# An attention stage rearranged: heads paired four apart, the spectrum stored mode-innermost, one cast moved to GpSimd, weight loads moved behind q, k, v

## The chip, the cores and the metric

The kernel runs on one core of a Trainium2 chip. The metric is device time in microseconds (us) for one execution; lower is better. A NeuronCore has a matrix engine (PE, TensorE), a vector engine (DVE, VectorE), an activation engine (ACT, ScalarE), GpSimd (POOL), a sync engine (SP) and sixteen DMA engines. Each engine takes its instructions in the order in which they were queued; an instruction that waits holds those behind it.

## The reference

Linear attention with phi(x) = elu(x) + 1, for 8 batches, 8 heads, 576 positions and 64 channels per head. Its output, laid out as 576 x 512 per batch, goes through a spectral mix: a real Fourier transform over positions, of which 64 modes are kept, a complex 512 x 512 matrix per mode, the inverse transform, and a residual channel product.

```python
q_p, k_p = (phi(q), phi(k))
kv = np.einsum('bhsd,bhse->bhde', k_p, v)
z = np.sum(k_p, axis=2)
num = np.einsum('bhsd,bhde->bhse', q_p, kv)
den = np.einsum('bhsd,bhd->bhs', q_p, z)[..., None] + 1e-06
x = (num / den)            # heads side by side: 512 channels

X = np.fft.rfft(x, axis=1)
Yr = einsum('bmd,mde->bme', Xr, w_r) - einsum('bmd,mde->bme', Xi, w_i)   # modes 0..63
Yi = einsum('bmd,mde->bme', Xr, w_i) + einsum('bmd,mde->bme', Xi, w_r)
y = np.fft.irfft(Y, n=S, axis=1)
u = x + y
return u + np.maximum(u @ w_ch, 0.0)
```

All inputs and the output are float32 in HBM. The weights w_r and w_i are 64 MB each.

## The kernel before, in words

**Attention stage, batch after batch.** Three loads on GpSimd's queue (line 141) bring k, q and v of a batch, cast to half precision on the way, into tiles of a pool with five buffers ("raw"). A tile is 128 partitions by four head pairs by 576: the 128 partitions hold two heads of 64 rows, and a head pair is two neighbouring heads. For k and for q, ACT takes the exponential in two halves (line 163), DVE makes max(x, 0) + 1 in place (line 164), and two DVE minima combine the two into phi (line 168). v is copied beside a column of ones (line 171). On PE, 36 small matmuls form k-transposed times v (kvp, line 182); ACT copies the wanted blocks (kvs, line 192); q is transposed in two groups of nine (line 204), each copied out by ACT (qT, line 209). For four groups of 128 positions and a tail of 64, PE forms numerator and denominator (num, line 228); DVE takes the reciprocal (line 235) and multiplies in two instructions of 256 columns (line 239) into the float32 tiles x_main and x_tail, which the kernel keeps to the end. ACT casts two groups at a time to half precision (line 248, 1024 columns) and the tail by itself (line 246). PE then applies the forward transform (xf, lines 254 and 257), and the spectrum goes into the tile xt_c.

**The spectrum tile.** xt_c is, for each of four channel groups, a run of modes; in a mode stand three sets of eight batches: minus the imaginary part (t = 0), the real part (t = 1) and the imaginary part (t = 2). DVE writes t = 1 and t = 2 (lines 260 and 261), ACT writes t = 0 with a factor of -1 (line 262). Each writes single elements 24 apart.

**Mode products.** For each mode two weight tiles (wr, wi, half a MB each when cast) are loaded (line 119). Eight matmuls multiply 32 neighbouring columns of xt_c, as the stationary operand, with 512 columns of weights (lines 319, 278 and 284). Of the 32 result rows of each channel group, sixteen count: `pick` selects them in a further matmul (lines 294 and 362). A stage tile (ystage, three buffers) takes the product out of PSUM.

**Weight buffers.** Modes 0 and 1 have a pool of four tiles, modes 2 to 6 the first use of a pool of ten; the load for mode 7 needs a buffer that the product of mode 2 hands back. Batch b of the attention stage issues the loads of mode b - 1, so that seven modes are asked for by batch 7; wch, the channel weights, follows (line 299).

**The rest.** Between the mode products, 36 channel products of x are made (line 340 on). At the end the inverse transform, the sums and the stores run (from line 415 on).

**The order of the work.** The program names an engine for each instruction. A planner sets the order of each engine's queue when the kernel is built, by program order and by its own estimate of when operands and buffers are ready; a load may thus stand ahead of one that comes earlier in the program. On the chip that order is fixed. PSUM has eight banks: three buffers of two banks ("big": kvp, the two transposes and num) and two for xf.

Of the kernel before, what the change touches and what calls it, by code (L numbers as in the profile page):

```python
# [20 lines left out]
def _dft_consts(S: int, NM: int):  # L21

    p = np.arange(NP)
    m = np.arange(NM)
    fwd = np.zeros((128, 5, 2 * NM), dtype=np.float64)
    s_cols = np.empty(S, dtype=np.int64)
    for jj in range(4):
        for j2 in range(2):
            s = NJ * p + 2 * jj + j2
            ang = 2.0 * np.pi * np.outer(s, m) / S  # L30
            fwd[j2 * 64 : j2 * 64 + 64, jj, :NM] = np.cos(ang)
            fwd[j2 * 64 : j2 * 64 + 64, jj, NM:] = -np.sin(ang)
# [12 lines left out]
    inv[:, 1, :] = -np.sin(ang) * scale[:, None]  # L45
    pick = np.zeros((128, 16), dtype=np.float16)
    for quad in range(4):
        for c in range(16):
            pick[quad * 32 + 8 + c, c] = 1.0
    return fwd.astype(np.float16), inv.reshape(2 * NM, S).astype(np.float16), pick  # L50


# [1 line left out]
def kernel(  # L54
# [10 lines left out]
    nc = tc.nc  # L65
# [4 lines left out]
    NHP = H // 2  # L70
    NDC = D // 128
    NJJ = 4
    SLOT = 3 * B
    XTW = 8 + NM * SLOT + 8
    NL = 8
    NE = NM - NL

# [27 lines left out]
        xpool.tile([128, D], F32, tag="x_tail", bufs=B // 2, name=f"x_tail{i}")  # L105
        for i in range(B // 2)
    ]
    xt_c = xpool.tile([128, NDC, XTW], BF16, name="xt_c")
    nc.vector.memset(xt_c[:, :, 0:8], 0.0)
    nc.vector.memset(xt_c[:, :, XTW - 8 : XTW], 0.0)  # L110
    xt_v = xt_c[:, :, 8 : 8 + NM * SLOT].rearrange("p c (m t b) -> p c m t b", t=3, b=B)

    W_KEEP = 10

# [21 lines left out]

    for b in range(B):
        raw = {}
        for nm, src in (("k", k), ("q", q), ("v", v)):
            t = sA.tile([128, NHP, NJ * Dh], F16, tag="raw", bufs=5, name=f"{nm}16_{b}")  # L140
            nc.gpsimd.dma_start(
                out=t,
                in_=src[b].rearrange("h s d -> (h s) d").rearrange(
                    "(hp r j) d -> r hp (j d)", r=128, j=NJ
                ),
            )
            raw[nm] = t
        if b >= 1:
            kk = b - 1
            if kk < n_pre:  # L150
                w_in[kk] = w_load(kk, wpre, "wp", W_PRE)
            else:
                w_in[kk] = w_load(kk, wpool, "w", W_KEEP)

        phi = {}
        for nm in ("k", "q"):

            e = sA.tile([128, 2, NJ, 2, Dh], F16, tag=f"{nm}e", bufs=2, name=f"{nm}e_{b}")
            ev = e.rearrange("p c j o d -> p c o j d")
            rf = raw[nm].rearrange("p a f -> p (a f)")  # L160
            rv = raw[nm].rearrange("p (c o) (j d) -> p c o j d", o=2, d=Dh)
            for c in range(2):
                nc.scalar.activation(out=ev[:, c], in_=rv[:, c], func=AF.Exp)  # L163
            nc.vector.tensor_scalar(  # L164
                out=rf, in0=rf, scalar1=0.0, scalar2=1.0, op0=ALU.max, op1=ALU.add
            )
            for c in range(2):
                nc.vector.tensor_tensor(out=ev[:, c], in0=ev[:, c], in1=rv[:, c], op=ALU.min)  # L168
            phi[nm] = e
# [48 lines left out]
        for jj in range(NJJ + 1):  # L218
# [3 lines left out]
            for hpp in range(2):  # L222
                for h2 in range(2):
                    for hpo in range(2):
# [8 lines left out]
            nv = num[orow, :, 0:260].rearrange("p o (c t n) -> p c o t n", c=2, t=2)  # L233
            rden = sA.tile([128, 2, 2, 2], F32, tag="rden", bufs=3, name=f"rd{b}_{jj}")
            nc.vector.reciprocal(out=rden[orow], in_=nv[:, :, :, :, 64])
            dst = xtl[orow, :] if tail else xm[:, jj, :]
            dv = dst.rearrange("p (c o t d) -> p c o t d", c=2, o=2, t=2)
            for hpp in range(2):
                nc.vector.tensor_tensor(
                    out=dv[:, hpp],  # L240
                    in0=nv[:, hpp, :, :, 0:64],
                    in1=rden[orow, hpp].unsqueeze(3).broadcast_to([64 if tail else 128, 2, 2, Dh]),
                    op=ALU.mult,
                )
            if tail:
                nc.scalar.copy(out=x16t[orow, :], in_=dst)
            elif jj % 2 == 1:
                nc.scalar.copy(out=x16[:, jj - 1 : jj + 1, :], in_=xm[:, jj - 1 : jj + 1, :])  # L248

        xf = psA.tile([128, NDC, 2, NM], F32, tag="xf", bufs=2, name=f"xf{b}")  # L250
        for dc in range(NDC):
# [5 lines left out]
            nc.tensor.matmul(  # L257
                o, x16t[half, dc::NDC], fwd_sb[half, NJJ, :], start=False, stop=True
            )
        nc.vector.tensor_copy(out=xt_v[:, :, :, 1, b], in_=xf[:, :, 0, :])  # L260
        nc.vector.tensor_copy(out=xt_v[:, :, :, 2, b], in_=xf[:, :, 1, :])
        nc.scalar.mul(out=xt_v[:, :, :, 0, b], in_=xf[:, :, 1, :], mul=-1.0)

    n_in = len(w_in)

# [6 lines left out]
    def mode_product(kk: int, ps, stage, yt_ps):  # L272
# [3 lines left out]
        for dc in range(NDC):  # L276
            quad = slice(dc * 32, dc * 32 + 32)
            nc.tensor.matmul(  # L278
                P[quad, :], xt_c[:, dc, 8 + kk * SLOT : 8 + kk * SLOT + 32], wr[:, dc, :],
                start=True, stop=False, tile_position=(0, dc * 32),  # L280
            )
        for dc in range(NDC):
            quad = slice(dc * 32, dc * 32 + 32)
            nc.tensor.matmul(  # L284
                P[quad, :], xt_c[:, dc, kk * SLOT : kk * SLOT + 32], wi[:, dc, :],
                start=False, stop=True, tile_position=(0, dc * 32),
            )
        st = stage.tile([128, D], F16, tag="ystage", bufs=3, name=f"ys{kk}")
        if kk % 2 == 0:
            nc.vector.tensor_copy(out=st, in_=P)  # L290
        else:
# [20 lines left out]
    for kk in range(n_pre):  # L312
        wr, wi = w_get(kk)
        P = psA.tile([128, D], F32, tag="xf", bufs=2, name=f"P{kk}")
        for t, w in ((0, wr), (1, wi)):
            for dc in range(NDC):
                quad = slice(dc * 32, dc * 32 + 32)
                c0 = kk * SLOT + (8 if t == 0 else 0)
                nc.tensor.matmul(
                    P[quad, :], xt_c[:, dc, c0 : c0 + 32], w[:, dc, :],  # L320
                    start=(t == 0), stop=(t == 1), tile_position=(0, dc * 32),
                )
        st = ystage0.tile([128, D], F16, tag="ystage", bufs=3, name=f"ys{kk}")
        if kk % 2 == 0:
            nc.vector.tensor_copy(out=st, in_=P)
        else:
# [169 lines left out]
```

## Time and profile before

| | |
|---|---|
| median of 3 runs | 487.29 us (486.23 to 487.69) |
| profiled execution: time | 487.18 us |
| profiled execution: span | 485.2 us |
| DVE busy | 171.2 us, 35% of the span |
| ACT busy | 163.5 us, 34% |
| PE busy, weight loads | 255.5 us (53%), 129.4 us (27%) |
| GpSimd busy | 108.6 us, 22% |
| DMA | 92.20 MB, mean 190 GB/s; GpSimd's queue 81.80 MB |
| chain that ended last | DMA 65%, issue 13%, DVE 8%, PE 7%, ACT 4% |

How to read the rows: a row of a timeline has the start in us from the span's start, the duration, the engine, the line, the operation, output and inputs with partitions x elements, the count, and in brackets the idle time of the engine before it with what ended it. A count over 1 merges neighbours; the duration is then that of all. A row of the groups ends in: busy us, mean ns of one | idle us before it and what ended most of it. A DMA issue row ends in KB and us from issue to landing. A row of one line of the kernel ends in the least, median and largest duration in ns, and the first and last start. The slice rows split the span into forty equal parts; a digit is the busy share in tenths, 9 for 90% or more.

### The profile page before, as it was taken

What the parts mean: (1) busy time and instruction counts of PE and PEld (TensorE: products, weight loads), DVE (VectorE), ACT (ScalarE), POOL (GpSimd) and SP (SyncE); (2) the same over time, 40 slices, a digit from 0 to 9 for tenths busy, and PEclk for the clock granted to TensorE, in tenths of its full rate; (3) what the DMA queues carried; (4) which work ended last, traced back from release to release, by engine and by line L of the source; (5) the groups of instructions that cost most, each with busy time, mean ns of one, the idle gap of its engine ahead of it and who ended that gap; (6) DMA issues with size and microseconds to landing.
All of it is one profiled execution on the core that took longest, in us unless ns stands there. A gap on an engine that the chain in (4) does not pass through costs nothing.

```text
span 485.2 us, 5542 instructions
## 1 busy us (share of the span) xinstructions
PE 255.5 (53%) x2156; PEld 129.4 (27%) x2156; DVE 171.2 (35%) x337; ACT 163.5 (34%) x227; POOL 108.6 (22%) x173
## 2 busy tenths in 40 slices
PE   0344576556747675677675433232323359429870
PEld 0333444434522322233332100010000028303320
DVE  1667667877452212211211101010110012116992
ACT  3657667874533434344334100000000002102320
POOL 3412313200003222222222222222222222003561
PEclk9957655565557979988979755555555559757996
DMA  9999999990006999999999999999999999962995
GB/s 160 211 209 209 209 211 209 211 209 17 1 0 121 213 214 213 213 214 213 214 213 214 213 214 214 213 213 212 215 212 215 212 215 211 215 124 75 283 274 171
DMA packets 37739, 92.20 MB, mean 190 GB/s; under 512 B 3537, under 2 KB 16593, under 8 KB 37713
## 3 DMA queue, kind: packets, MB, share of 16 engines
q0 software_dynamic: 31632, 81.80, 86.9%
q1 hardware_dynamic: 3328, 5.20, 3.6%
q10 hardware_dynamic: 2752, 4.85, 3.2%
q8 instruction: 17, 0.28, 0.2%
q14 instruction: 10, 0.07, 0.0%
HBM read 163.93 MB, written 9.44 MB: 357 GB/s over the span
## 4 chain that ended last, share of the span: by engine, by line
DMA 65%; issue 13%; DVE 8%; PE 7%; ACT 4%; POOL 0%; POOLq 0%; SPq 0%; DVEq 0%
DMA q_3_640<-in_q_dram 4%; DMA wi_3418<-in_moe_w_i_dram 4%; DMA wr_2621<-in_moe_w_r_dram 4%; DMA wr_3283<-in_moe_w_r_dram 4%; DMA wr_3109<-in_moe_w_r_dram 4%; DMA wr_2988<-in_moe_w_r_dram 4%; DMA wr_2865<-in_moe_w_r_dram 4%; DMA wr_2500<-in_moe_w_r_dram 4%; DMA wr_2256<-in_moe_w_r_dram 4%; DMA wr_2133<-in_moe_w_r_dram 4%; DMA wr_2012<-in_moe_w_r_dram 4%; DMA wr_2744<-in_moe_w_r_dram 4%; DMA wr_2377<-in_moe_w_r_dram 4%; DMA wr_1889<-in_moe_w_r_dram 4%; DMA k_5_998<-in_k_dram 4%
## 5 line engine op out<-in xcount | busy, mean ns | idle before, releaser
L284 PEld LDWEIGHTS <-xt_c 128*32 128x32 bf16 x248 | 11.8, 101 | 86.1 <-issue 84.9
L278 PEld LDWEIGHTS <-xt_c 128*32 128x32 bf16 x248 | 9.0, 98 | 44.9 <-issue 17.9
L119 POOL DMA_DIRECT2D wr_1732<-in_moe_w_r_dram x1 | 0.5, 543 | 51.0 <-PE P_1627 L278 51.0
L182 PE MATMUL kvp_121<-vpad_100,ke_108 64*128 64x130 f16 x36 | 2.1, 308 | 15.2 <-DVE vpad_100 L171 15.2
L382 PEld LDWEIGHTS <-YT 128*112 128x112 f16 x32 | 7.7, 288 | 2.7 <-issue 2.2
L441 POOL TENSOR_TENSOR x_main_76<-x_main_76,r_3474 128x512 f32<-128x512 f32 x1 | 1.3, 1267 | 29.6 <-ACT r_3474 L440 29.6
L388 PEld LDWEIGHTS <-YT 128*112 128x112 f16 x32 | 7.5, 294 | 0.5
L182 PEld LDWEIGHTS <-ke_108 64*128 64x128 f16 x36 | 2.0, 141 | 15.1 <-DVE ke_108 L168 12.6
L424 PEld LDWEIGHTS <-inv_sb 128*128 128x128 f16 x32 | 3.2, 100 | 8.7 <-issue 6.6
L419 PEld LDWEIGHTS <-id_64 128*128 128x128 f16 x36 | 3.5, 100 | 6.4 <-issue 2.1
L423 PEld LDWEIGHTS <-inv_sb 128*128 128x128 f16 x32 | 3.3, 102 | 4.8 <-issue 1.7
L163 ACT ACTIVATE ke_108<-k_0_102 128x1152 f16<-128x1152 f16 x2 | 2.2, 1154 | 6.5 <-DMA k_0_102<-in_k_dram 6.5
L254 PE MATMUL xf_254<-fwd_sb,x_0_184 128*128 128x128 f16 x16 | 2.2, 263 | 4.0 <-ACT x_0_184 L248 4.0
L164 DVE TENSOR_SCALAR k_0_102<-k_0_102 128x2304 f16<-128x2304 f16 x1 | 0.8, 759 | 9.9 <-ACT ke_108 L163 9.9
L163 ACT ACTIVATE ke_468<-k_2_458 128x1152 f16<-128x1152 f16 x2 | 2.3, 1160 | 5.6 <-DMA k_2_458<-in_k_dram 5.6
L292 ACT CAST ys_3429<-P_3420 128x512 f16<-128x512 f32 x1 | 0.6, 586 | 10.4 <-PE P_3420 L284 10.4
L290 DVE CAST ys_3410<-P_3401 128x512 f16<-128x512 f32 x1 | 0.7, 691 | 9.4 <-PE P_3401 L284 9.4
L163 ACT ACTIVATE ke_828<-k_4_818 128x1152 f16<-128x1152 f16 x2 | 2.7, 1326 | 3.9 <-DMA k_4_818<-in_k_dram 3.9
L290 DVE CAST ys_2810<-P_2801 128x512 f16<-128x512 f32 x1 | 0.7, 692 | 9.1 <-PE P_2801 L284 9.1
L290 DVE CAST ys_3122<-P_3113 128x512 f16<-128x512 f32 x1 | 0.7, 691 | 9.1 <-PE P_3113 L284 9.1
L290 DVE CAST ys_2931<-P_2922 128x512 f16<-128x512 f32 x1 | 0.7, 692 | 9.1 <-PE P_2922 L284 9.1
L290 DVE CAST ys_2687<-P_2678 128x512 f16<-128x512 f32 x1 | 0.7, 691 | 9.1 <-PE P_2678 L284 9.1
(1293 smaller groups left out, 844.5 us busy)
## 6 DMA issues: line engine op xcount, KB each, us to landing
k_0_102<-in_k_dram POOLq DMA_DIRECT2D x1, 576.0 KB, 7.5
q_0_104<-in_q_dram POOLq DMA_DIRECT2D x1, 576.0 KB, 9.4
v_0_106<-in_v_dram POOLq DMA_DIRECT2D x1, 576.0 KB, 11.5
k_1_278<-in_k_dram POOLq DMA_DIRECT2D x1, 576.0 KB, 13.6
q_1_280<-in_q_dram POOLq DMA_DIRECT2D x1, 576.0 KB, 15.7
v_1_282<-in_v_dram POOLq DMA_DIRECT2D x1, 576.0 KB, 9.2
k_2_458<-in_k_dram POOLq DMA_DIRECT2D x1, 576.0 KB, 14.7
q_2_460<-in_q_dram POOLq DMA_DIRECT2D x1, 576.0 KB, 15.7
```

Of the source, the lines that this page charges most:

```text
L163: nc.scalar.activation(out=ev[:, c], in_=rv[:, c], func=AF.Exp)
L182: nc.tensor.matmul(kv_ps[:, h2, hpp * 130 : hpp * 130 + 130], kp[rows, hpp, j].rearrange("p o d -> p (o d)"), vp[rows, 2 * hpp : 2 * hpp + ...
L254: nc.tensor.matmul(o, x16[:, jj, dc::NDC], fwd_sb[:, jj, :], start=(jj == 0), stop=False)
L278: nc.tensor.matmul(P[quad, :], xt_c[:, dc, 8 + kk * SLOT : 8 + kk * SLOT + 32], wr[:, dc, :], start=True, stop=False, tile_position=(0, dc ...
L284: nc.tensor.matmul(P[quad, :], xt_c[:, dc, kk * SLOT : kk * SLOT + 32], wi[:, dc, :], start=False, stop=True, tile_position=(0, dc * 32),)
L290: nc.vector.tensor_copy(out=st, in_=P)
L382: nc.tensor.matmul(z_ps[: 2 * NE, :], lhs, wch16[:, ec, :], start=(ec == 0), stop=(ec == NDC - 1),)
L388: nc.tensor.transpose(y_ps[: 2 * NE, ec * 128 : ec * 128 + 128], lhs, id16)
L419: nc.tensor.matmul(e, id16, E0[t], start=True, stop=False, skip_group_check=True)
L423: nc.tensor.matmul(y, lhs, YZ[b][:, 0, :])
L424: nc.tensor.matmul(e, lhs, YZ[b][:, 1, :], start=False, stop=True, skip_group_check=True)
L441: nc.gpsimd.tensor_tensor(out=x, in0=x, in1=r, op=ALU.add)
```

## The change

Four things in the attention stage and one in what reads the spectrum.

1. Heads are paired four apart: the pair (c, o) is head pair c plus two times o, where it was two times c plus o. Views of the raw tiles and of v change accordingly. In num, the eight heads then stand so that one DVE multiplication of 512 columns writes a whole group of positions.
2. The cast of x to half precision (128 x 512 per group of positions) is issued to GpSimd, one group at a time, instead of to ACT for two groups. The tail's cast stays on ACT.
3. xt_c is stored with the mode as the innermost index: group, t, batch, mode. One DVE copy writes t = 1 and t = 2 together in runs of 64; ACT's negation writes runs of 64. The 32 stationary columns of a mode are now 64 elements (128 bytes) apart; a pad of 1024 elements at the end is cleared. `pick` moves by eight rows.
4. q is loaded and processed ahead of k. Weight loads are issued in batches 2, 4 and 6 only (modes 0, 1, 2); those of modes 3 to 6 come in the loop behind wch that was there already.
5. ystage has two buffers instead of three.

```diff
-    SLOT = 3 * B
-    XTW = 8 + NM * SLOT + 8
+    XDC = 3 * B * NM
+    XTW = NDC * XDC + 2 * B * NM
...
-    xt_c = xpool.tile([128, NDC, XTW], BF16, name="xt_c")
-    nc.vector.memset(xt_c[:, :, 0:8], 0.0)
-    nc.vector.memset(xt_c[:, :, XTW - 8 : XTW], 0.0)
-    xt_v = xt_c[:, :, 8 : 8 + NM * SLOT].rearrange("p c (m t b) -> p c m t b", t=3, b=B)
+    xt_c = xpool.tile([128, XTW], BF16, name="xt_c")
+    nc.vector.memset(xt_c[:, NDC * XDC : XTW], 0.0)
+    xt_v = xt_c[:, 0 : NDC * XDC].rearrange("p (c t b m) -> p c t b m", c=NDC, t=3, b=B)
+
+    def xt_cols(dc: int, t: int, kk: int):
+
+        c0 = dc * XDC + t * B * NM + kk
+        return xt_c[:, c0 : c0 + 31 * NM + 1 : NM]
...
-        for nm, src in (("k", k), ("q", q), ("v", v)):
+        for nm, src in (("q", q), ("k", k), ("v", v)):
...
-        if b >= 1:
-            kk = b - 1
+        if b % 2 == 0 and b > 0:
+            kk = b // 2 - 1
...
-        for nm in ("k", "q"):
+        for nm in ("q", "k"):
...
-            rv = raw[nm].rearrange("p (c o) (j d) -> p c o j d", o=2, d=Dh)
+            rv = raw[nm].rearrange("p (o c) (j d) -> p c o j d", o=2, d=Dh)
...
-                        vp[rows, 2 * hpp : 2 * hpp + 2, j, 0:65],
+                        vp[rows, hpp::2, j, 0:65],
...
-            for hpp in range(2):
-                nc.vector.tensor_tensor(
-                    out=dv[:, hpp],
-                    in0=nv[:, hpp, :, :, 0:64],
-                    in1=rden[orow, hpp].unsqueeze(3).broadcast_to([64 if tail else 128, 2, 2, Dh]),
-                    op=ALU.mult,
-                )
+            nc.vector.tensor_tensor(
+                out=dst.rearrange("p (o c d) -> p o c d", o=2, c=4),
+                in0=nv[:, :, :, 0:64],
+                in1=rden[orow].unsqueeze(3).broadcast_to([64 if tail else 128, 2, 4, Dh]),
+                op=ALU.mult,
+            )
             if tail:
                 nc.scalar.copy(out=x16t[orow, :], in_=dst)
-            elif jj % 2 == 1:
-                nc.scalar.copy(out=x16[:, jj - 1 : jj + 1, :], in_=xm[:, jj - 1 : jj + 1, :])
+            else:
+                nc.gpsimd.tensor_copy(out=x16[:, jj, :], in_=dst)
...
-        nc.vector.tensor_copy(out=xt_v[:, :, :, 1, b], in_=xf[:, :, 0, :])
-        nc.vector.tensor_copy(out=xt_v[:, :, :, 2, b], in_=xf[:, :, 1, :])
-        nc.scalar.mul(out=xt_v[:, :, :, 0, b], in_=xf[:, :, 1, :], mul=-1.0)
+        nc.vector.tensor_copy(out=xt_v[:, :, 1:3, b, :], in_=xf)
+        nc.scalar.mul(out=xt_v[:, :, 0, b, :], in_=xf[:, :, 1, :], mul=-1.0)
...
-                P[quad, :], xt_c[:, dc, 8 + kk * SLOT : 8 + kk * SLOT + 32], wr[:, dc, :],
+                P[quad, :], xt_cols(dc, 1, kk), wr[:, dc, :],
...
-                P[quad, :], xt_c[:, dc, kk * SLOT : kk * SLOT + 32], wi[:, dc, :],
+                P[quad, :], xt_cols(dc, 0, kk), wi[:, dc, :],
...
-        st = stage.tile([128, D], F16, tag="ystage", bufs=3, name=f"ys{kk}")
+        st = stage.tile([128, D], F16, tag="ystage", bufs=2, name=f"ys{kk}")
```

More of the change, by code (lines that the diff above doesn't have):

```diff
@@ L48, in _dft_consts @@
         for c in range(16):
-            pick[quad * 32 + 8 + c, c] = 1.0
+            pick[quad * 32 + c, c] = 1.0
     return fwd.astype(np.float16), inv.reshape(2 * NM, S).astype(np.float16), pick
@@ L232 @@
                         )
[L233 to L235 removed]
+            nv = num[orow, :, 0:260].rearrange("p o (c n) -> p o c n", c=4)
+            rden = sA.tile([128, 2, 4], F32, tag="rden", bufs=3, name=f"rd{b}_{jj}")
+            nc.vector.reciprocal(out=rden[orow], in_=nv[:, :, :, 64])
             dst = xtl[orow, :] if tail else xm[:, jj, :]
[L237 to L244 removed]
+            nc.vector.tensor_tensor(
[4 more added lines that the diff above has]
+            )
             if tail:
                 nc.scalar.copy(out=x16t[orow, :], in_=dst)
[L247 to L248 removed]
+            else:
+                nc.gpsimd.tensor_copy(out=x16[:, jj, :], in_=dst)
         xf = psA.tile([128, NDC, 2, NM], F32, tag="xf", bufs=2, name=f"xf{b}")
@@ L317 @@
                 quad = slice(dc * 32, dc * 32 + 32)
-                c0 = kk * SLOT + (8 if t == 0 else 0)
                 nc.tensor.matmul(
-                    P[quad, :], xt_c[:, dc, c0 : c0 + 32], w[:, dc, :],
+                    P[quad, :], xt_cols(dc, 1 - t, kk), w[:, dc, :],
                     start=(t == 0), stop=(t == 1), tile_position=(0, dc * 32),
                 )
-        st = ystage0.tile([128, D], F16, tag="ystage", bufs=3, name=f"ys{kk}")
+        st = ystage0.tile([128, D], F16, tag="ystage", bufs=2, name=f"ys{kk}")
         if kk % 2 == 0:
```

## The prediction

> **What bounds the kernel now.** I read the page first: its forty slices, then the group with the longest idle time.
>
> ```profile
> span 485.2 us, 5542 instructions
> DMA  9999999990006999999999999999999999962995
> L119 POOL DMA_DIRECT2D wr_1732<-in_moe_w_r_dram x1 | 0.5, 543 | 51.0 <-PE P_1627 L278 51.0
> ```
>
> The DMA engines are full except for a hole of three slices of 12.1 us. The hole ends with the load wr_1732, which waits for a product of mode 2 to hand back a weight buffer. So I read the GpSimd queue and the DMA issues around it.
>
> ```profile
> 97.15 0.75 POOL L141 DMA_DIRECT2D v_7_1362<-in_v_dram  x1 [4.65 <-issue]
> 148.86 0.54 POOL L119 DMA_DIRECT2D wr_1732<-in_moe_w_r_dram  x1 [50.96 <-PE P_1627 L278]
> ...
> v_7_1362<-in_v_dram POOLq DMA_DIRECT2D x1, 576.0 KB, 14.0
> wr_1732<-in_moe_w_r_dram POOLq DMA_DIRECT2D x1, 512.0 KB, 5.1
> ```
>
> The last load before the hole lands at 97.15 + 14.0 = 111.15. By then all q, k, v, wch and seven modes' weights are in, and every weight buffer is taken. Nothing moves until the attention stage ends and the products of modes 0 to 2 run. After that the chain of waits is DMA, load after load:
>
> ```profile
> 160.50 19.13 DMA wr_1889<-in_moe_w_r_dram
> ...
> 180.16 19.13 DMA wr_2012<-in_moe_w_r_dram
> ```
>
> Eight loads go by between the first two issues: 19.66 / 8 = 2.46 us for one. This stretch keeps its length whatever the attention stage does. So the span moves one for one with the issue of wr_1732, now at 148.86. A hole closed entirely would put wr_1732's own 2.46 us behind 111.15, instead of landing at 148.86 + 5.1: a gain of 40.4, the floor at 487.2 - 40.4 = 446.8.
>
> The question is then what the attention stage takes. Its spectrum matmuls close each batch:
>
> ```profile
> L257 PE MATMUL xf_254<-fwd_sb,x16t_185 x4: 244/245/292, 36.1 to 37.9; 64*128 64x128 f16 x4
> ...
> L257 PE MATMUL xf_1334<-fwd_sb,x16t_1265 x4: 291/292/307, 125.5 to 127.9; 64*128 64x128 f16 x4
> ...
> L257 PE MATMUL xf_1514<-fwd_sb,x16t_1445 x4: 291/292/295, 138.4 to 140.7; 64*128 64x128 f16 x4
> ```
>
> Batch 0 ends at 38.1, batch 6 at 128.2, batch 7 at 141.0: 14.7 us a batch on average, but 12.9 for the last, when no load is outstanding. The ACT timeline has the difference:
>
> ```profile
> 8.73 2.21 ACT L163 ACTIVATE ke_108<-k_0_102 128x1152 f16<-128x1152 f16 x2 [6.50 <-DMA k_0_102<-in_k_dram]
> 11.54 2.22 ACT L163 ACTIVATE qe_114<-q_0_104 128x1152 f16<-128x1152 f16 x2 [0.59 <-DMA q_0_104<-in_q_dram]
> ...
> 30.78 1.16 ACT L163 ACTIVATE ke_468<-k_2_458 128x1152 f16<-128x1152 f16 x1 [5.63 <-DMA k_2_458<-in_k_dram]
> 31.84 1.03 ACT L248 CAST x_0_184<-x_main_76 128x1024 f16<-128x1024 f32 x1
> ```
>
> ACT holds at the exponential of k of batch b+2 until that tensor lands, and batch b's cast to half precision stands behind it. The tensors land 11.54 - 8.73 = 2.81 us apart.
>
> **The change part by part.** I follow the last batch, from the end of xf_1334 (128.15):
>
> ```profile
> 128.19 1.33 DVE L260 CAST xt_c<-xf_1334 128x256 bf16<-128x256 f32 x1 [4.11 <-PE xf_1334 L257]
> ...
> 133.42 0.21 DVE L235 RECIPROCAL rd_0_1455<-num_0_1446 128x8 f32<-128x8 f32 x1 [2.72 <-PE num_0_1446 L228]
> ...
> 133.66 0.76 DVE L239 TENSOR_TENSOR x_main_83<-num_0_1446,rd_0_1455 128x256 f32<-128x256 f32 x2
> ```
>
> ```profile
> 128.22 0.75 ACT L192 CAST kvs_1418<-kvp_1381 64x260 f16<-64x260 f32 x2 [3.44 <-PE xf_1334 L257]
> 129.32 1.12 ACT L209 COPY qT_1421<-qTp_0_1422 128x1152 f16<-128x1152 f16 x1 [0.34 <-PE qTp_0_1422 L204]
> 130.73 1.34 ACT L262 ACTIVATE xt_c<-xf_1334 128x256 bf16<-128x256 f32 x1 [0.29 <-DVE xt_c L261]
> 131.55 1.47 ACT L209 COPY qT_1421<-qTp_1_1433 128x1152 f16<-128x1152 f16 x1
> ...
> 136.68 1.04 ACT L248 CAST x_7_1444<-x_main_83 128x1024 f16<-128x1024 f32 x1 [0.47 <-DVE x_main_83 L239]
> 137.75 0.62 ACT L246 CAST x16t_1445<-x_tail_87 64x512 f16<-64x512 f32 x1
> 143.66 1.34 ACT L262 ACTIVATE xt_c<-xf_1514 128x256 bf16<-128x256 f32 x1 [5.30 <-DVE xt_c L261]
> 147.61 0.62 ACT L342 CAST x16w_1687<-x_main_76 128x512 f16<-128x512 f32 x1
> ```
>
> Spectrum stored mode-innermost. Lines 260, 261 and 262 now write every 24th element; they become one DVE copy and one ACT negation of contiguous runs. The nearest rows are these, and the one above for L192 (0.37 for 260 columns):
>
> ```profile
> L290 DVE CAST ys_3410<-P_3401 128x512 f16<-128x512 f32 x1 | 0.7, 691 | 9.4 <-PE P_3401 L284 9.4
> L441 POOL TENSOR_TENSOR x_main_76<-x_main_76,r_3474 128x512 f32<-128x512 f32 x1 | 1.3, 1267 | 29.6 <-ACT r_3474 L440 29.6
> L284 PEld LDWEIGHTS <-xt_c 128*32 128x32 bf16 x248 | 11.8, 101 | 86.1 <-issue 84.9
> L382 PEld LDWEIGHTS <-YT 128*112 128x112 f16 x32 | 7.7, 288 | 2.7 <-issue 2.2
> ```
>
> So 0.69 and 0.37. The copy ends by 128.9, and the negation fits ahead of 129.32 instead of between the two qT copies. The second qT copy starts at 130.35 instead of 131.55: 1.2 us off the chain in each batch. Behind the last batch the way from 141.03 to the first product (145.05, below) shrinks from 4.0 to 0.05 + 0.69 + 0.37 + 0.1 = 1.2.
>
> The price is that the 32 stationary columns lie 128 bytes apart. The strided load of 112 columns took 288 ns; in proportion 32 columns are 82, under the 101 of today. If a strided load cost 288 whatever its width, six groups of four before wr_1732's release would grow by 4.3 us. I take 0.3, near the proportional end.
>
> ```profile
> 145.05 0.62 PE L319 MATMUL P_1542<-wr_284,xt_c 128*32 128x512 bf16 x4 [4.02 <-ACT xt_c L262]
> ...
> 443.84 1.19 DVE x_main_76 L437 x2
> ```
>
> Heads paired four apart. Two multiplications of 256 columns become one of 512. Two now take 0.76 together (the row at 133.66), in part overlapped with what follows; one of 512 with a PSUM input takes 1.19 / 2 = 0.595. Saved is between 0 and 0.16 each; I take 0.07, 0.3 a batch of five. The strided v operand leaves 36 matmuls of 130 columns: nothing.
>
> Cast on GpSimd. Two ACT casts of about 1.0 leave; four GpSimd casts of 512 columns come. No row shows one: ACT's 0.62 for that shape below, GpSimd's two-input 1267 ns above. I take 1.0, nearer the row of its own engine. They start when the first multiplication ends: 133.66 - 1.2 + 0.6 = 133.05. With one load issue of 0.75 between them, the fourth ends at 133.05 + 4.0 + 0.75 = 137.8, against 136.68 + 1.04 = 137.7 now. The ACT tail cast moves from 138.4 to 136.9 and stops being the last input. The spectrum matmuls end 2.6 behind the last input: 140.4. A batch is then 12.25.
>
> The Trainium skill's GPSIMD Engine Reference, section 3.1, puts a best-case loop over 512 elements at 769 ns; by that the fourth cast would end at about 136.9, level with the tail cast, and the sum would be near the first rival's.
>
> Queue of the casts. Behind a cast on GpSimd stand the loads of batches b+2 and b+3, and behind those the exponentials. The queue already waits longer than four casts:
>
> ```profile
> 36.73 0.77 POOL L141 DMA_DIRECT2D v_3_642<-in_v_dram  x1 [9.55 <-DVE ke_468 L168]
> ...
> 77.35 0.57 POOL L119 DMA_DIRECT2D wr_1364<-in_moe_w_r_dram  x1
> 83.03 0.76 POOL L141 DMA_DIRECT2D v_6_1182<-in_v_dram  x1 [5.12 <-ACT kvs_878 L192]
> ```
>
> A raw buffer frees only after the multiplications in DVE's order, so I cost this at nothing; without that cover it is 4 us on a batch's loads.
>
> Weights queued behind. Three modes instead of seven come before the last v. From v_0 at 8.73 + 2 x 2.81 = 14.4, v_7 lands at 14.4 + 21 x 2.81 + 6 x 2.46 = 88.2 instead of 111.15, or 10.5 a batch, under 12.25. So ACT's waits for data, the excess of 14.7 over 12.9, should go. The nine loads then behind (four modes, wch) take 22 us and end at 111 if the queue never idles: covered until 125. If issued late they are a rival. q ahead of k costs nothing, because kvp needs v, still third; at most 2.8 once.
>
> The rest: two stage buffers instead of three are refilled one mode (4.9 us) apart, nothing, at most 1 us in the seven early products; the larger memset falls in DVE's idle start.
>
> The sum. Batch 0's first multiplication starts at 26.04:
>
> ```profile
> 26.04 0.76 DVE L239 TENSOR_TENSOR x_main_76<-num_0_186,rd_0_195 128x256 f32<-128x256 f32 x2
> ```
>
> It ends 0.6 later; 4.75 for the casts and 2.6 for the matmuls make 34.0. Seven batches of 12.25: 119.8. To the first product 1.2; from it to wr_1732 148.86 - 145.05 = 3.8, plus 0.3: 125.1. Gain 23.8. The profiled execution took 487.18, 2.0 beside its span and 0.1 under the median of 487.29; so 463.4.
>
> **The rivals.**
> Data pace (0.17): casts at ACT's 0.62, so that the tail cast at 136.9 decides, 0.9 sooner in each of eight batches: 125.1 - 7.2 = 117.9, gain 31.0: 456. For it: ACT and DVE are lighter. Against: POOL's 1267.
>
> Weights stuck (0.10): the nine loads are issued behind the last cast at 119.8 - 2.6 = 117.2. With 2.6 of start-up (5.1 - 2.46) and 22, wr_1732 moves from 142.0 instead of 151.5: gain 9.5, 478. For it: one in-order queue. Against: nothing makes these loads wait for a buffer, and a weight load did overtake a waiting v (wr_1364 above).
>
> Order as now (0.15): the planner lets weights overtake, as wr_1364 of batch 7 passed v_6. v_7 lands near 111 and the attention ends between one batch behind that (123.4) and today's 29.9 less 1.2 (139.8). Plus 5.3 to wr_1732: gain 20 to 4; I take 12, 475.
>
> Mutual blocking (0.10, the slower side): GpSimd casts and DVE's half-precision instructions with all operands in SBUF exclude each other. A batch holds seven of those, 0.76 each (two of line 164, four of 168, one of 171):
>
> ```profile
> L168 DVE TENSOR_TENSOR ke_108<-ke_108,k_0_102 128x1152 f16<-128x1152 f16 x2 | 1.4, 755 | 0.0
> ...
> 51.55 0.76 DVE L171 COPY vpad_100<-v_3_642 128x2304 f16<-128x2304 f16 x1
> ...
> 51.50 1.11 POOL L141 DMA_DIRECT2D v_4_822<-in_v_dram  x1 [7.50 <-ACT x_1_364 L248]
> ```
>
> For it: this issue took 1.11 instead of 0.75 beside such a copy. Against: most casts run beside multiplications, which read PSUM. Fully blocked, 5.3 us replace the 0.75: 4.55 more in each of eight batches, 125.1 + 36.4 = 161.5: 500. It loses from 3.7 us blocked per batch on (0.75 + 23.8 / 8). The Trainium skill's SBUF — State Buffer, section "Who interferes with whom", states the rule: the shared port is an exclusive lock; this one row agrees.
>
> **How the numbers follow.** The forecast has 0.48, with 454 to 473 of its own: the upper cast price (1.27) is 1.1 a batch, 9 in all, and as much the other way. Data pace, stuck weights and order as now lie between 450 and 484; blocking lies above. The range is 450 to 484. A change under 0.3% (1.5 us) can't be told from none. Faster 0.87, same 0.04, slower 0.09.
>
> **What would show it.** The hole in the slices shrinks from three to one or two; wr_1732 issued near 125; v_7 landing near 88; casts near 1.0; xt_c by DVE near 0.7; no ACT wait for data beyond batch 1. Casts over 1.9, waits of casts for DVE, or loads idle behind casts make it wrong.

## The result: 470.81 us, and the profile after

| | before | after |
|---|---|---|
| median | 486.89 us (4 runs) | 470.81 us (4 runs, 469.51 to 472.53) |
| ratio | 1 | 0.9671, 95% interval 0.9636 to 0.9707 |
| profiled execution: time, span | 487.18, 485.2 us | 471.04, 469.2 us |
| load that ends the DMA hole, issued at | 148.86 us | 132.22 us |
| spectrum of batches 0 and 7 complete | 38.1, 141.0 us | 33.8, 127.1 us |
| mean batch period | 14.7 us | 13.33 us |

The change gains 16.1 us; the forecast was 23.8. The time lies in the range.

On the page of the changed kernel, the DMA slices of 11.7 us:

```profile
DMA  9999999995069999999999999999999999943985
```

The hole is shorter, but it is still there. GpSimd's queue in the timeline shows the loads ahead of it, the last of which is wi_1504, and the one that ends it (wr_1699 is what wr_1732 was before). The table of DMA issues gives the time to landing in its last column:

```profile
72.09 0.99 POOL L300 DMA_DIRECT2D wch_68<-in_moe_w_ch_dram  x1
...
76.22 0.55 POOL L123 DMA_DIRECT2D wr_1490<-in_moe_w_r_dram  x1
...
82.22 1.02 POOL L145 DMA_DIRECT2D k_7_1319<-in_k_dram  x1
...
83.80 0.54 POOL L123 DMA_DIRECT2D wi_1492<-in_moe_w_i_dram  x1
85.69 1.12 POOL L145 DMA_DIRECT2D v_7_1321<-in_v_dram  x1 [1.34 <-ACT kvs_1025 L196]
...
101.43 0.55 POOL L123 DMA_DIRECT2D wi_1504<-in_moe_w_i_dram  x1
...
132.22 0.54 POOL L123 DMA_DIRECT2D wr_1699<-in_moe_w_r_dram  x1 [8.74 <-PE P_1594 L279]
```

```profile
k_7_1319<-in_k_dram POOLq DMA_DIRECT2D x1, 576.0 KB, 10.0
v_7_1321<-in_v_dram POOLq DMA_DIRECT2D x1, 576.0 KB, 11.8
```

wr_1699 is issued 16.64 us earlier and the span is 16.0 us shorter: the span did move one for one with this issue. But wch and the two weights of mode 3 (wr_1490, wi_1492) stand ahead of v_7, although the program has them behind it. v_7 lands at 85.69 + 11.8 = 97.5.

The batches by DVE's spectrum copy, which starts when a batch's spectrum matmuls are done (batches 0, 5, 6 and 7):

```profile
33.81 0.69 DVE L262 CAST xt_c<-xf_250 128x512 bf16<-128x512 f32 x1 [1.64 <-PE xf_250 L259]
...
104.98 0.69 DVE L262 CAST xt_c<-xf_1118 128x512 bf16<-128x512 f32 x1 [1.32 <-PE xf_1118 L259]
...
116.01 0.69 DVE L262 CAST xt_c<-xf_1294 128x512 bf16<-128x512 f32 x1 [3.84 <-PE xf_1294 L259]
...
127.13 0.69 DVE L262 CAST xt_c<-xf_1466 128x512 bf16<-128x512 f32 x1 [3.35 <-PE xf_1466 L259]
```

Two speeds: (104.98 - 33.81) / 5 = 14.23 us a batch while loads come, 11.03 and 11.12 for the last two, when no load is awaited. The list of ACT's waits says what the first five wait for. Before (waits for k between 20 and 150 us; us in total, times, longest):

```profile
ACT ke_468 L163 <- DMA k_2_458<-in_k_dram: 5.6, 1, 5.6
ACT ke_828 L163 <- DMA k_4_818<-in_k_dram: 3.9, 1, 3.9
ACT ke_1008 L163 <- DMA k_5_998<-in_k_dram: 3.1, 1, 3.1
ACT ke_1368 L163 <- DMA k_7_1358<-in_k_dram: 2.8, 1, 2.8
ACT ke_1188 L163 <- DMA k_6_1178<-in_k_dram: 1.6, 1, 1.6
```

And after, the same stretch:

```profile
ACT ke_1329 L167 <- DMA k_7_1319<-in_k_dram: 7.0, 1, 7.0
ACT ke_809 L167 <- DMA k_4_795<-in_k_dram: 4.9, 1, 4.9
...
ACT ke_981 L167 <- DMA k_5_971<-in_k_dram: 3.7, 1, 3.7
```

ACT waited 17.0 us for k; it now waits 17.8 (four more rows, of 0.7, 0.6, 0.6 and 0.3, are left out). Its waits for q went from 1.2 to 2.4 us. What a wait for k holds, in ACT's timeline and then in PE's:

```profile
84.52 0.75 ACT L196 CAST kvs_1025<-kvp_988 64x260 f16<-64x260 f32 x2 [0.33 <-PE kvp_988 L186]
92.28 1.16 ACT L167 ACTIVATE ke_1329<-k_7_1319 128x1152 f16<-128x1152 f16 x1 [7.01 <-DMA k_7_1319<-in_k_dram]
93.46 1.12 ACT L213 COPY qT_1028<-qTp_0_1029 128x1152 f16<-128x1152 f16 x1
```

```profile
87.81 0.50 PE L208 MATMUL qTp_0_1029<-id_64,qe_975 128*128 128x128 f16 x3
```

k of batch 7 lands at 92.2 and its exponential stands ahead of the qT copy of batch 5. The operand of that copy needs nothing from batch 7, and PE has it ready at 88.3. ACT stands still for 7.0 us, and batch 5 for some 5 of them, because of a tensor used two batches later.

### The profile page after: what moved, and what is told of

The parts are those of the page before. It is cut to its first block, busy times and chain, and to the rows that moved or that the text cites. A ratio compares the mean times of both kernels' runs of the same rounds, so it can differ in the third digit from the quotient of the medians.

```text
span 469.2 us, 5483 instructions
## 1 busy us (share of the span) xinstructions
PE 261.8 (56%) x2156; PEld 139.6 (30%) x2156; DVE 156.6 (33%) x288; ACT 140.9 (30%) x211; POOL 128.7 (27%) x205
## 4 chain that ended last, share of the span: by engine, by line
DMA 63%; PE 15%; DVE 10%; ACT 6%; issue 2%; POOL 2%; POOLq 0%; ACTq 0%; SPq 0%
DMA wi_3385<-in_moe_w_i_dram 4%; DMA wr_2310<-in_moe_w_r_dram 4%; DMA wr_3076<-in_moe_w_r_dram 4%; DMA wr_2955<-in_moe_w_r_dram 4%; DMA wr_2832<-in_moe_w_r_dram 4%; DMA wr_2588<-in_moe_w_r_dram 4%; DMA wr_2467<-in_moe_w_r_dram 4%; DMA wr_3250<-in_moe_w_r_dram 4%; DMA wr_2711<-in_moe_w_r_dram 4%; DMA wr_2187<-in_moe_w_r_dram 4%; DMA wr_2066<-in_moe_w_r_dram 4%; DMA wr_1943<-in_moe_w_r_dram 4%; DMA wr_1822<-in_moe_w_r_dram 4%; DMA k_1_275<-in_k_dram 3%; DMA k_4_795<-in_k_dram 2%
## 5 line engine op out<-in xcount | busy, mean ns | idle before, releaser
L285 PEld LDWEIGHTS <-xt_c 128*32 128x32 bf16 x248 | 18.0, 154 | 82.0 <-issue 80.7
L279 PEld LDWEIGHTS <-xt_c 128*32 128x32 bf16 x248 | 13.7, 157 | 43.5 <-issue 17.6
L186 PE MATMUL kvp_120<-vpad_99,ke_113 64*128 64x130 f16 x36 | 2.1, 309 | 16.1 <-DVE ke_113 L172 16.1
L186 PEld LDWEIGHTS <-ke_113 64*128 64x128 f16 x36 | 1.9, 141 | 16.1 <-DVE ke_113 L172 16.1
L250 POOL CAST x_5_1051<-x_main_81 128x512 f16<-128x512 f32 x4 | 2.4, 622 | 9.5 <-DVE x_main_81 L241 9.5
L250 POOL CAST x_7_1399<-x_main_83 128x512 f16<-128x512 f32 x4 | 2.4, 616 | 9.1 <-DVE x_main_83 L241 9.1
L250 POOL CAST x_6_1227<-x_main_82 128x512 f16<-128x512 f32 x4 | 2.4, 618 | 7.7 <-DVE x_main_82 L241 7.7
L250 POOL CAST x_2_531<-x_main_78 128x512 f16<-128x512 f32 x4 | 2.4, 618 | 4.9 <-DVE x_main_78 L241 4.9
```

The source lines that it names most:

```text
L186: nc.tensor.matmul(kv_ps[:, h2, hpp * 130 : hpp * 130 + 130], kp[rows, hpp, j].rearrange("p o d -> p (o d)"), vp[rows, hpp::2, j, 0:65], s ...
L250: nc.gpsimd.tensor_copy(out=x16[:, jj, :], in_=dst)
L279: nc.tensor.matmul(P[quad, :], xt_cols(dc, 1, kk), wr[:, dc, :], start=True, stop=False, tile_position=(0, dc * 32),)
L285: nc.tensor.matmul(P[quad, :], xt_cols(dc, 0, kk), wi[:, dc, :], start=False, stop=True, tile_position=(0, dc * 32),)
```

## The experiments

The kernel before had a median of 487.0 to 487.2 us beside each of the experiments. The theories: **A**, the order of the loads sets the stage, k is late because weights stand ahead of it; **B**, the casts in GpSimd's queue hold the loads back; **C**, the place of the weights is worth nothing; **D**, the savings in the chain of a batch add up in every batch.

### Weights held back for certain

All fourteen weight loads and wch behind the last v:

```diff
-        if b % 2 == 0 and b > 0:
-            ...  (loads of modes 0, 1, 2)
...
+    with tc.issue_after(last_v.ins):
+        while n_in < n_pre + W_KEEP // 2:
+            ...  (loads of modes 0 to 6)
+        nc.gpsimd.dma_start(out=wch16, ...)
```

> The changed kernel with every weight load and wch queued behind the last v load. Theory A (the DMA stream's order sets the attention stage: k of batch b+2 arrives late because weights stand ahead of it in the stream, and ACT holds batch b for it): ACT's waits for k_4, k_5 and k_7 (4.9, 3.7 and 7.0 us in the changed kernel) shrink to under 1 each, a batch takes 11 to 11.7 us, the last spectrum matmul ends near 113 instead of 127; the time is 458 to 463, bounded by the fifteen loads that now come after v_7. Theory B (the casts in GpSimd's queue hold the loads back, and they arrive late for that): the loads stay behind the casts, the waits stay at 3 to 7 us, and as the weights come later besides, the time is 470 to 475.

466.91 us, ratio 0.9598 (0.9576 to 0.962). The milder version holds back only the nine loads of wch and modes 3 to 6, as the program text of the change has them:

```diff
-    nc.gpsimd.dma_start(out=wch16, ...)
-    while n_in < n_pre + W_KEEP // 2:
-        ...
+    with tc.issue_after(last_v.ins):
+        nc.gpsimd.dma_start(out=wch16, ...)
+        while n_in < n_pre + W_KEEP // 2:
+            ...
```

> The changed kernel with only wch and the loads of modes 3 to 6 queued behind the last v load; in the changed kernel wch and one load of mode 3 overtook q_7, k_7 and v_7. Theory A: k_7 lands two loads earlier (4.9 us: near 87.4 instead of 92.3), the last spectrum matmul ends near 122, and the time is about 466. Theory B: k_7 still lands near 90 or later and the time stays within 1.5 us of 470.8.

468.63 us, 0.9624 (0.9604 to 0.9644); this overlaps the interval of the changed kernel and can't quite be told from it. ACT's waits for k fall from 17.8 to 13.1 us, about what two loads of 2.46 us less ahead of k_7 are worth:

```profile
ACT ke L168 <- DMA k<-in_k_dram: 13.1, 6, 4.9
```

Both stay short of what A expected. In the first, k is awaited for 7.1 us instead of 17.8, yet the batches come 12.54 us apart, from 34.49 to 122.26:

```profile
34.49 0.69 DVE L257 CAST xt_c<-xf 128x512 bf16<-128x512 f32 x1 [2.84 <-PE xf L254]
50.84 0.69 DVE L257 CAST xt_c<-xf 128x512 bf16<-128x512 f32 x1 [1.59 <-PE xf L254]
...
122.26 0.69 DVE L257 CAST xt_c<-xf 128x512 bf16<-128x512 f32 x1 [3.36 <-PE xf L254]
```

Batch 1 takes 16.35 us, 4.8 of them in a wait for k of batch 3. The six behind it come (122.26 - 50.84) / 6 = 11.9 us apart with a single wait for k, of 1.0 us: there the data was in time, and something else holds the batch.

### One part undone

Casts back on ACT, in pairs as before:

```diff
-            else:
-                nc.gpsimd.tensor_copy(out=x16[:, jj, :], in_=dst)
+            elif jj % 2 == 1:
+                nc.scalar.copy(out=x16[:, jj - 1 : jj + 1, :], in_=xm[:, jj - 1 : jj + 1, :])
```

> The changed kernel with the cast back on ACT, two groups at a time as before. Theory A: the loads land as fast as the DMA engines carry them, as in the changed kernel, so ACT's waits for k are no shorter, and the cast stands behind them again: 474 to 479. Theory B: with no cast in GpSimd's queue the loads are issued 3 to 6 us earlier and land so; ACT's waits shrink, and the time is 466 to 471.

471.87 us, 0.9689 (0.9674 to 0.9703): not to be told from the changed kernel, and between the two bands expected. The planner let weights overtake still more; wch now left at 53.55 instead of 72.09. ACT's waits moved from k to q: 11.0 us for q, 1.9 for k.

Weight loads again in every batch from 1 on:

```diff
-        if b % 2 == 0 and b > 0:
-            kk = b // 2 - 1
+        if b >= 1:
+            kk = b - 1
```

> The changed kernel with the weight loads where they were before: one mode in each batch from the second on. Theory A: seven modes stand in the stream ahead of the last tensors, k_7 lands near 100 as before instead of 92, and everything behind it moves along: about 479. Rival C (the gain came from the lighter instructions alone and the place of the weights is worth nothing): within 1.5 us of 470.8.

473.65 us, 0.9723 (0.9703 to 0.9743): 2.8 us lost by the medians, with an interval that just touches that of the changed kernel. That is neither A's 479 nor C's nothing.

The old spectrum layout in the changed kernel (with `pick`, the pads and the matmul operands as before):

```diff
-        nc.vector.tensor_copy(out=xt_v[:, :, 1:3, b, :], in_=xf)
-        nc.scalar.mul(out=xt_v[:, :, 0, b, :], in_=xf[:, :, 1, :], mul=-1.0)
+        nc.vector.tensor_copy(out=xt_v[:, :, :, 1, b], in_=xf[:, :, 0, :])
+        nc.vector.tensor_copy(out=xt_v[:, :, :, 2, b], in_=xf[:, :, 1, :])
+        nc.scalar.mul(out=xt_v[:, :, :, 0, b], in_=xf[:, :, 1, :], mul=-1.0)
```

> The changed kernel with the old spectrum layout: three strided copies behind each spectrum matmul instead of two contiguous ones; pairing, cast on GpSimd and load order as changed. Alone, the layout took 6.5 us off. Parts add up: 470.8 + 6.5 = 477 (476 to 479). Parts need each other (the layout lets ACT and DVE reach the next k in time, so that without it the other three are worth no more than alone, 0 to +2.5): 484 to 490. Layout hidden behind the waits for k (these decide in the changed kernel): 471 to 473.

479.92 us, 0.9847 (0.9814 to 0.988): the layout is worth 9.1 us beside the other parts. The time lies between the two bands expected, for parts that add up and for parts that need each other.

### One part alone, in the kernel before

The spectrum layout alone (the reverse of the edit just shown, with two ystage buffers):

> The kernel before with the spectrum stored mode-innermost and nothing else (two stage buffers, as the larger tile needs). Theory D (each batch is a chain of instructions, and what is taken off it counts in every batch): 1.2 us in each of seven batches and 2.8 behind the last, 11 in all: about 476. Theory A in its strong form (the data stream holds batches 0 to 5, so that only the last two and the end gain): 1.2 twice and 2.8, 5 in all: about 482. Either way the strided stationary loads take about 155 ns, as in the changed kernel, and cost nothing beside the DMA stream.

480.46 us, 0.9871 (0.9854 to 0.9889), between D's 476 and A's 482. The casts on GpSimd alone:

```diff
-            elif jj % 2 == 1:
-                nc.scalar.copy(out=x16[:, jj - 1 : jj + 1, :], in_=xm[:, jj - 1 : jj + 1, :])
+            else:
+                nc.gpsimd.tensor_copy(out=x16[:, jj, :], in_=dst)
```

> The kernel before with the cast of x issued to GpSimd, group by group, and nothing else. The cast back on ACT cost the changed kernel 1.1 us, within what can be told. Theory D: 0 to 2 us faster. A rival, that the cast behind ACT's waits for k was what held the kernel before: 5 us faster or more (ACT waited 5.6, 3.9, 3.1, 1.6 and 2.8 us for k). A second rival, that casts in GpSimd's queue hold back the loads: slower by 2 us or more.

487.02 us, 0.9996 (0.9986 to 1.0007): nothing, so neither of D's two rivals came true. The order alone:

```diff
-        for nm, src in (("k", k), ("q", q), ("v", v)):
+        for nm, src in (("q", q), ("k", k), ("v", v)):
...
-        if b >= 1:
-            kk = b - 1
+        if b % 2 == 0 and b > 0:
+            kk = b // 2 - 1
...
-        for nm in ("k", "q"):
+        for nm in ("q", "k"):
```

> The kernel before with q loaded and processed ahead of k and the weights loaded in batches 2, 4 and 6 only, and nothing else. The changed kernel lost 2.8 us when the weights went back to each batch. Theory D: 2 to 4 us faster. Theory A in its strong form: the stage is freed of ACT's waits for data (17 us in all for k of batches 2 to 7), 8 us faster or more.

489.49 us, 1.0064 (1.0039 to 1.0089): slower by 2.5. The pairing alone:

```diff
-            rv = raw[nm].rearrange("p (c o) (j d) -> p c o j d", o=2, d=Dh)
+            rv = raw[nm].rearrange("p (o c) (j d) -> p c o j d", o=2, d=Dh)
...                             (v's operand, and one multiplication instead of two)
```

> The kernel before with heads paired four apart and one multiplication of 512 columns, and nothing else. Theory D: 0.07 us for each of five groups, 0.3 in a batch, 2 to 2.5 in all: about 485. Rival: nothing within 1.5 us of the kernel before.

487.35 us, 1.001 (1.0001 to 1.002): nothing, as the rival had it.

Alone, the parts bring -6.5, 0.0, +2.5 and +0.4 us, together -3.6; the whole change brings -16.1. The order alone misses by both theories because the queue didn't take the order of the program: in the trace all fourteen weight loads and wch are issued before v_7 in spite of the program text. v_7 leaves at 98.81, later than the 97.15 of before, and ACT's waits for k grow to 22.3:

```profile
98.81 0.75 POOL L141 DMA_DIRECT2D v<-in_v_dram  x1 [6.04 <-issue]
```

```profile
ACT ke L163 <- DMA k<-in_k_dram: 22.3, 7, 7.5
```

Held to its word, with all weights behind v_7 as in the first experiment, the order alone in the kernel before becomes:

> The kernel before with the order q, k, v and with all fourteen weight loads and the channel weights held back until v_7's load is issued, so that the order is kept without the casts in GpSimd's queue; layout, pairing and cast as before. If late data alone holds the old stage: waits for k gone, stage end some 8 us earlier, 477 to 480. If the old stage is held by its own chain (three strided copies, ACT's casts, order k before q): waits gone but the batch stays at 14 to 15 us, 486 to 489.

481.25 us, 0.9871 (0.9854 to 0.9889). That is 8.2 us less than the order alone and 5.9 less than the kernel before, and the waits for k fall to 5.8:

```profile
ACT ke L158 <- DMA k<-in_k_dram: 5.8, 6, 2.2
```

The batches then come (135.47 - 35.82) / 7 = 14.24 us apart, by the starts of DVE's first spectrum copy: with data in time, the old chain holds. The time is below the 486 to 489 that was expected with such a batch: batch 0 ends 2.3 us earlier than before (35.82 against 38.15), and seven batches of 14.24 instead of 14.70 are 3.2 us.

### Order kept, casts on ACT

The first experiment's kernel with the casts back on ACT (the edit shown above):

> The version with all weights behind v_7 (466.9 us), but the x16 casts back on ACT, in pairs as before. If the cast on GpSimd served only to keep the order of the loads: 466.9 within 1. If it also shortens the batch (ACT freed of two casts of some 1 us each, one of them ahead of the spectrum matmul): 8 x 0.5 to 1 us more, 471 to 475.

459.35 us, 0.9425 (0.9411 to 0.9439): 7.6 us faster than with the casts on GpSimd, which neither reading had expected.

```profile
36.25 0.69 DVE L257 CAST xt_c<-xf 128x512 bf16<-128x512 f32 x1 [1.50 <-PE xf L254]
48.42 0.69 DVE L257 CAST xt_c<-xf 128x512 bf16<-128x512 f32 x1 [2.25 <-PE xf L254]
...
115.56 0.69 DVE L257 CAST xt_c<-xf 128x512 bf16<-128x512 f32 x1 [3.45 <-PE xf L254]
```

11.33 us a batch instead of 12.54, though batch 0 ends 1.8 us later. ACT's waits between 20 and 128 us show what differs, first with the casts on GpSimd, then on ACT:

```profile
ACT x16t L243 <- DVE x_tail L236: 22.9, 7, 4.4
ACT ke L162 <- DMA k<-in_k_dram: 7.1, 4, 4.8
```

```profile
ACT qT L208 <- PE qTp L203: 10.0, 6, 2.3
...
ACT ke L162 <- DMA k<-in_k_dram: 1.2, 2, 0.6
```

With the casts gone from its queue, ACT comes early to the tail's cast and waits 22.9 us there in all, for the last multiplication of each batch; the exponentials of the next k stand behind it. With the casts on ACT, the same time holds casts and exponentials. One place shows it best. Casts on GpSimd (k of batch 3, then qT of batch 1):

```profile
37.09 2.21 ACT L162 ACTIVATE ke<-k 128x1152 f16<-128x1152 f16 x2 [4.83 <-DMA k<-in_k_dram]
...
39.61 2.14 ACT L208 COPY qT<-qTp 128x1152 f16<-128x1152 f16 x2
```

Casts on ACT:

```profile
33.87 1.12 ACT L208 COPY qT<-qTp 128x1152 f16<-128x1152 f16 x1
...
39.92 1.16 ACT L162 ACTIVATE ke<-k 128x1152 f16<-128x1152 f16 x1
```

The load of k_3 is issued at 25.66 in one and 25.65 in the other. Its place in ACT's queue differs: ahead of batch 1's qT copies, or behind them. Batch 1 takes 16.35 us in one and 12.17 in the other, 4.2 of the 8.5 us between the two kernels in seven batches; the other 4.3 are spread over the batches behind it, and no single wait was found for them. The granted TensorE clock between 36 and 116 us differs as well, 0.54 against 0.62; as the four runs of the first experiment don't become faster with their clock (last section), it is not a likely cause. That the order differs and that the wait goes with it is shown; that the planner chose the first order because it thought the tensor would be there is an inference.

Beside the kept order, layout and pairing are worth 481.25 - 459.35 = 21.9 us, where alone they brought 6.5 and nothing. The reading is that they shorten the chain, and that only here is the chain all that holds.

### The spectrum written one batch later

The first experiment's kernel (casts on GpSimd) with the spectrum matmuls of a batch written behind the transposes and qT copies of the next one:

```diff
+    pend = None
     for b in range(B):
...                             (loads, phi, kvp, kvs, transposes, qT copies)
+        if pend is not None:
+            spectrum(*pend)     # xf, xt_c of batch b - 1
...                             (num, multiplications, casts)
-        xf = psA.tile(...)      # xf, xt_c of batch b
+        pend = (b, x16, x16t)
+    spectrum(*pend)
```

> The version with all weights behind v_7 (466.9 us), with the spectrum matmul of batch b written behind the q transposes and qT copies of batch b+1, so that those don't stand behind it on TensorE and ACT. If the chain from batch to batch sets the 12.5 us: the transposes (1.9 to 2.1 us) and two copies (1.1 each) leave the chain, 10.5 to 11.2 us a batch, where data arrival takes over: 457 to 461. If ACT and DVE are held by their own work or by the loads: 465 to 468. If the later spectrum delays the last batch: 468 to 470.

453.36 us, 0.9303 (0.9281 to 0.9325): the fastest kernel of all. The batches come (104.69 - 34.55) / 7 = 10.02 us apart, below the band expected. ACT's waits for k are nearly gone, and the DMA engines have no hole left (the GB/s row has the same forty slices as the DMA row, here 11.3 us each):

```profile
34.55 0.69 DVE L153 CAST xt_c<-xf 128x512 bf16<-128x512 f32 x1 [1.12 <-PE xf L150]
...
104.69 0.69 DVE L153 CAST xt_c<-xf 128x512 bf16<-128x512 f32 x1 [3.35 <-PE xf L150]
```

```profile
ACT ke L178 <- DMA k<-in_k_dram: 2.4, 6, 0.7
```

```profile
GB/s 155 207 208 180 132 208 205 200 214 213 212 213 213 213 213 213 214 213 214 215 213 213 213 214 214 213 213 213 213 214 213 213 213 215 214 40 145 283 274 158
```

Here the rule of one for one ends. In the thirteen other kernels of this document the profiled span is 336.0 to 337.0 us longer than the time at which the load behind mode 2's product is issued. Here that load is issued at 109.79 and the span is 452.1, 342.3 more: the load leaves 17.6 us earlier than in the first experiment (127.35), and the span gains only 11.7. From 57 us until the last weights the stream of loads runs without a gap, so it is what limits the kernel now. Its own gap is early, at 180 and 132 GB/s between 34 and 57 us; against the 208 beside it that is an estimated 5.7 us of loading.

This kernel too has four casts a batch in GpSimd's queue ahead of loads, and its batches are the shortest; in the first experiment GpSimd stood idle for 2.0 to 3.3 us between the last cast of a batch and the next load of q, k or v. B is not what holds the stage in either. What may hold the batches next is DVE, busy for 22.61 of 24 us between 36 and 60 us, by the windows of this run:

```profile
36.00:60.00 24.00, 18.10 (x289) 14.04 (x289) 22.61 (x45) 18.11 (x23) 15.05 (x19) 0.72 0.99 159
```

(The columns are length, busy time and count of PE, weight loads, DVE, ACT and GpSimd, the granted clock, DMA share and GB/s.) The same edit with the casts on ACT was not run.

## Why the prediction was right and where it fell short

**One for one: right.** 16.64 us of issue, 16.0 of span, and it held in every kernel but the last.

**Batch 0, and the way behind the last batch: right.** Batch 0's spectrum is there at 33.8 against 34.0. From the copy's start at 127.13 to the first product it takes 1.2 us, as forecast, and from there to wr_1699 132.22 - 128.29 = 3.9, against 4.1:

```profile
128.29 0.68 PE L319 MATMUL P_1509<-wr_451,xt_c 128*32 128x512 bf16 x4 [1.20 <-ACT xt_c L263]
```

**The layout's rows: right.** The copy takes 0.69 us, the negation 0.38 to 0.40. The strided stationary loads cost more each than 82 ns in proportion, but far from 288 (at which the 24 loads would have added 4.5 us, a little more than the 4.3 of the prediction):

```profile
L285 PEld LDWEIGHTS <-xt_c 128*32 128x32 bf16 x248 | 18.0, 154 | 82.0 <-issue 80.7
L279 PEld LDWEIGHTS <-xt_c 128*32 128x32 bf16 x248 | 13.7, 157 | 43.5 <-issue 17.6
...
L250 POOL CAST x_5_1051<-x_main_81 128x512 f16<-128x512 f32 x4 | 2.4, 622 | 9.5 <-DVE x_main_81 L241 9.5
```

**The cast's price: mis-sized.** 0.62 us instead of the 1.0 taken from a two-input row, at the lower bound. So the condition of the rival "Data pace" held, and in the last two batches its effect shows: 11.03 and 11.12 us, where 12.25 was forecast and 11.35 followed from that rival. But the 456 us it gave didn't come, for the next reason. The Trainium skill's GPSIMD Engine Reference, section 3.1, has 769 ns for a best-case loop over 512 elements; the cast here is faster than that, and the measurement decides.

**The step that failed: "So ACT's waits for data, the excess of 14.7 over 12.9, should go."** They stayed, 17.0 us before and 17.8 after, and the batches with loads take 14.23 us instead of 12.25. Five batches at 14.23 and two at 11.07 make 93.3 us; seven at 12.25 made 85.75. The 7.6 us between them are the whole miss: 125.1 + 7.6 = 132.7, and wr_1699 is issued at 132.22. The step had two faults.

First, v_7 was to land at 88.2 with six weight loads ahead of it. Nine were, and three loads at 2.46 are 7.4: 95.6, of the 97.5 measured. That is the mechanism of the rival "Order as now": it came true for three loads of nine, and the result, a gain of 16.1, lies between the forecast's 23.8 and that rival's 12. But the overtaking explains the lesser part of the waits: the two loads that got ahead of k_7 are 4.9 of its 7.0 us, and with them held back 13.1 of the 17.8 us stayed. Holding all weights back lowered the waits for k to 7.1 us and brought 3.9 us by the medians.

Second, the pace of the data was compared with a batch as if any ACT instruction could go when its operand is there. The place of the instruction in the queue counts. k_4 landed at 50.4 and k_5 at 64.2, where the prediction's own pace puts them (14.4 + 11 x 2.81 + 2 x 2.46 = 50.2 and 14.4 + 14 x 2.81 + 4 x 2.46 = 63.6). No load had overtaken them, and ACT still waited 4.9 and 3.7 us, because their exponentials stood ahead of the qT copies of batches 2 and 3. The order alone, kept, left a batch of 14.24 us; with the shorter chain and the casts on ACT it was 11.33; with the spectrum written later, 10.02. (The pace of 10.5 had six weight loads in it; with none ahead of v_7, as in these three, the same sum gives 21 x 2.81 / 7 = 8.4.)

**The cast on GpSimd: counted as neutral in the chain, and it is not.** The prediction put the fourth cast at 137.8 against 137.7 and the tail's cast 1.5 us earlier. Once the loads stay in order, the kernel with the casts on GpSimd is 7.6 us slower, about half of it through the place of one exponential in ACT's queue. In the kernel as changed this can't be seen (471.87 against 470.81). There, with the casts on ACT, more weights overtake (twelve and wch ahead of v_7 instead of eight and wch): the casts in GpSimd's queue seem to have a side use in keeping loads back. That these two cancel fits all four kernels, with and without kept order, but the share of each inside the changed kernel was not measured.

**The queue of the casts at nothing.** k_4 is issued at 38.93, between casts of batch 1, and k_7 at 82.22, between those of batch 4. But the DMA engines didn't run dry for it. Before and after, by the slices of the page:

```profile
GB/s 160 211 209 209 209 211 209 211 209 17 1 0 121 213 214 213 213 214 213 214 213 214 213 214 214 213 213 212 215 212 215 212 215 211 215 124 75 283 274 171
GB/s 160 207 211 208 210 203 208 209 200 102 1 122 212 214 212 213 214 214 213 214 214 214 213 213 213 213 214 214 213 213 213 214 214 214 213 82 107 285 272 166
```

The second to the eighth slice have 209.9 GB/s on average before and 208.0 after, 0.9% of 82 us: an estimated 0.7 us of loading. A price of nothing was near enough.

**Weights stuck: did not happen.** The last of the nine loads leaves at 101.43, before the last two batches' casts.

**Mutual blocking: there, and small.** DVE's in-place maximum took 1.3 us instead of 0.7 where it ran beside casts (71.48 beside casts from 69.33 to 72.16):

```profile
L168 DVE TENSOR_SCALAR q_5_969<-q_5_969 128x2304 f16<-128x2304 f16 x1 | 1.3, 1301 | 0.0
L168 DVE TENSOR_SCALAR q_7_1317<-q_7_1317 128x2304 f16<-128x2304 f16 x1 | 1.3, 1294 | 0.0
...
L168 DVE TENSOR_SCALAR q_6_1141<-q_6_1141 128x2304 f16<-128x2304 f16 x1 | 0.7, 701 | 0.0
```

That is 0.6 us in two of eight batches, and in three others the pair of DVE minima beside a cast took 1.70 us instead of 1.42; full blocking was 4.55 in each batch. By the rule of the Trainium skill's SBUF — State Buffer, section "Who interferes with whom", the port is an exclusive lock; these rows agree with it in kind, and most casts run beside multiplications from PSUM, as the prediction had it.

## What to carry to other kernels

Where a planner orders the queues, a program text that puts loads last is a wish: read the issue order in the trace, and force it where it matters (8.2 us here). In an in-order queue the question for each wait is not only when the operand comes, but what stands behind it; a long wait of ACT that holds an earlier batch's work was mended here by order (13.6 us for the spectrum written one batch later), not by freeing the engine. A tensor that comes in time by its mean pace can still come late for the place of its reader: compare time by time. Parts that shorten a chain showed little while data held the stage and more when it didn't (layout and pairing: 6.5 us alone, 21.9 with the order kept), so test them after the wait is gone.

## What the runs showed of the hardware that was not expected

GpSimd's cast of 128 x 512 from float32 to half precision took 0.62 us, as long as ACT's cast of 64 x 512 (0.60 to 0.62), though its two-input instruction of that width takes 1.27. Stationary columns 128 bytes apart cost 154 and 157 ns per load of 32 against 101 and 98 side by side, with no visible effect on the time: from the load behind mode 2's product to the end it is 336.1 to 336.6 us in the kernels with the old layout, 336.0 to 337.0 in those with the new one (the last experiment aside). In the four runs of the first experiment the mean granted TensorE clock was 0.694, 0.799, 0.809 and 0.693, and the times were 465.64, 466.41, 468.65 and 467.41 us: the time does not follow the clock here.
